# Chunked attention and a squared-ReLU FFN on one core: the opening's copies, loads and products, the mixes and bursts, and the last block's pieces are placed anew

## The chip, the cores and the metric

The kernel runs on one core of one Trainium2 chip. The time is that of one execution of the program on the device, in microseconds (us); the median of several executions is compared. In the rows PE is the matrix engine (PEld its weight loads), DVE the vector engine, ACT the scalar engine, POOL the GpSimd engine, and SP a sequencer that only issues transfers. ACT and POOL issue transfers too.

## The reference

```
q_c, k_c, v_c = (x.reshape(B, H, nc, 64, D) for x in (q, k, v))   # B, H, S, D = 8, 8, 576, 64
scores = np.matmul(q_c, k_c.transpose(0, 1, 2, 4, 3)) / np.sqrt(D)
attn = np.exp(scores - scores.max(-1, keepdims=True))
attn = attn / (attn.sum(-1, keepdims=True) + 1e-9)
x = np.matmul(attn, v_c)  ->  (4608 tokens, 512)
h = x @ w_in                                                       # 512 -> 2048
g = np.where(h >= 1, h, np.where(h <= -1, 0, (h + 1) ** 2 / 4))
out = g @ w_out                                                    # 2048 -> 512
```

Inputs and output are float32.

## The kernel before

**Tiles.** The 4608 tokens are nine tiles `t` of 512. Attention is done for two heads (a pair `g`, four to a tile) at a time: `q` and `k` are turned so that the head dimension lies on the partitions, the scores of the pair go to PSUM, DVE and ACT make the softmax, the result is turned back, and the product with `v` gives one 128-row slice of `x`. Each operand of the FFN is split into a high part and a low part (`xh` and `xl`, `gh` and `gl`, two halves of each weight), and each product is three matrix products: high by high, high by low, low by high. A product of 512 columns is the unit of the work.

**Three stages.** The opening handles tile 0: for each of its four pairs `attn_turn` (two PE transposes of 128x512 and a copy each from PSUM to SBUF), `attn_products(scores_of)`, `attn_softmax` (maximum, difference, exponential, sum, and on POOL the multiplication by the inverse sum), `attn_turn_back`, `attn_products(values_of)` and `attn_split` (ACT writes `xh`, DVE writes `xl`). The weights arrive as 64-bit words and `prepare` turns one of them into two parts with three ACT and two DVE instructions; its first ACT instruction (`Prelu`) waits for the load. Until data is there, PE multiplies the identity by itself (`warm`). Tiles 0 to 2 (`PAIRED`) then run the FFN as it stands, 16 blocks of 12 products with `w_in` and 12 with `w_out` to a tile. Blocks are numbered over the three tiles, so that block 36 is block 4 of tile 2. Tiles 3 to 8 run two at a time with seven products in place of eight (`ffn_quad`, `ffn_mixed_out`); their mixed weights are made beforehand by `mix_weights` ("mixes": DVE sums, ACT copies and seven stores to DRAM by POOL) and streamed back by POOL.

**Bursts.** The attention of later tiles is computed in bursts of two pairs. A burst is the values of one couple of pairs and the scores of the next in one group of 64x64 products. Between two bursts lies a chain: maximum, difference, exponential, sum, multiplication, a DVE transpose into `qT_both`, an SP move of `qT_both` to `aT_both` by four transfers, and DVE transposes of the next `k` and `q`. The one that writes `qT_both` cannot start before the move has read it. `PAIRS` says behind which blocks of tiles 0 to 2 a burst stands, `SCHEDULE` behind which block a mix stands and in which scratch.

**Who orders the work.** `Plan.add` collects each piece of work with an engine, an assumed duration, the buffers that it reads and writes, and an assumed delay of a transfer. `Plan.emit` runs its own estimate of all engines and writes every engine's instructions in the order that comes out, with due times counted back from the end as the rank. On the chip each engine takes its instructions in just that order.

**The end.** The last output block is made by `ffn_mixed_out` with `ending` set. Its 512 tokens go in two pieces of 256: for each piece 24 products, then per half (`c`) a DVE addition of the sum kept in SBUF (`total_of`), a DVE transpose, and four stores, two from SP and two from ACT:

```python
LAST_BANKS = a_banks, h_banks
for e, c, k in itertools.product(range(2), range(2), range(PARTS)):
    if ending:
        last_product(LAST_BANKS[e][c], k, c, slice(e * T // 2, (e + 1) * T // 2), ...)
```

Of the kernel before, what the change touches and what calls it, by code (L numbers as in the profile page):

```python
# [19 lines left out]
class Wires:  # L20


    def __init__(self):
        self.now = 0.0
        self.queues = {"pool": deque(), "sp": deque()}
        self.asked = []
# [36 lines left out]
class Plan:  # L63
# [14 lines left out]
    def __init__(self):  # L78
        self.parts = []
        self.writer = {}  # L80
        self.readers = {}
        self.written = {}
        self.behind = 0
        self.rank = []
        self.early = {}

    def add(
        self, engine, cost, emit, reads=(), writes=(), lag=0.0, columns=0, sends=0, kb=0, run=0, after=None,
    ):
        n = len(self.parts)  # L90
        needs = {self.writer[k] for k in (*reads, *writes) if k in self.writer}
# [61 lines left out]
    def run(self, filler, live):  # L153
# [33 lines left out]
        done = {None}  # L187

# [8 lines left out]
        while left or sending:  # L197
# [44 lines left out]
            n = heapq.heappop(now[e])[1]  # L242
            left -= 1
# [5 lines left out]
            times[n], self.took[n] = start, end - start  # L249
            if e == "sp":  # L250
# [5 lines left out]
            for m in range(sends):  # L256
                wires.begin(start + cost * (m + 1) / sends, "pool" if e == "pool" else "sp", n, *wire)
# [4 lines left out]
def kernel(  # L262
# [35 lines left out]
    EARLY = 2  # L298
# [12 lines left out]
        (15, EARLIER), (15, EARLIER), (15, EARLIER), (17, EARLIER), (19, OWN), (22, EARLIER), (23, RING5), (25, RING5), (28, OWN), (33, OWN), (36, LATER), (39, LATER), (41, OWN), (41, RING5), (45, RING5), (46, OWN),  # L311
# [101 lines left out]

    def load_weight(w, j):
        def emit():
            words[w, j] = dst = place("words", w, j, [P, 2 * T], U32)
            if w == "wi":
                nc.sync.dma_start(
# [5 lines left out]
            else:  # L424
                nc.sync.dma_start(out=dst, in_=w_out[j * P:(j + 1) * P, :])

        plan.add("sp", 0.57, emit, (), (f"{w}{j}_0", f"{w}{j}_1"), lag=2.5,
# [3 lines left out]
    def prepare(w, j):  # L431
# [23 lines left out]
        plan.add("dve", 0.6, join, both, (ykey,))  # L455
# [20 lines left out]
        plan.add("dve", 0.6, low, (ykey, both[0]), (both[1],))  # L476
# [50 lines left out]
    def load_heads(t, g, which="qkv"):  # L527
        for n, src, bufs in (("q", q, q_bufs), ("k", k, k_bufs), ("v", v, v_bufs)):
# [5 lines left out]
            if BATCH[t] is None:  # L534
                parts *= 2

            issuer, queue = ("act", nc.scalar) if (n, t) == ("k", 0) and g < 2 else ("sp", nc.sync)
            plan.add(
                issuer, (0.67 if t < 2 else 0.55) * parts,
# [10 lines left out]

    def attn_turn(t, g):
        for n, (name, bufs, src_bufs, dst_bufs) in enumerate(
# [6 lines left out]
            turned[n] = plan.add(  # L559
                "act", 0.48, lambda ps=ps, dst=dst: nc.scalar.copy(out=dst, in_=ps), (pkey,), (dkey,)  # L560
            )
# [85 lines left out]
    def attn_softmax(t, g):  # L647
# [26 lines left out]
        plan.add("pool", 1.05, lambda: nc.gpsimd.tensor_tensor(  # L674
# [838 lines left out]
```

## Time and profile before

| | before |
|---|---|
| median of 3 runs (lowest, highest) | 793.46 us (792.54, 793.69) |
| the profiled execution | 793.6 us |
| its span from first to last instruction | 791.8 us |
| PE busy in the span | 782.8 us (99%) |
| DVE, ACT, POOL busy | 659.9, 523.4, 178.4 us |
| granted clock of PE over the span | 0.999 of full speed |

The time holds 1.8 us beside the span. PE is busy almost throughout, but in the first 25 us much of that is `warm`, and a busy PE may also be waiting inside an instruction; so the distance between the starts of products says more than the busy time.

### The profile page before, as it was taken

To read this page: it belongs to the slowest core of one execution; us is meant where nothing else is said; L and a number is where in the kernel's file an instruction comes from. 1 tells how busy PE (TensorE), PEld (TensorE's weight loads), DVE (VectorE), ACT (ScalarE), POOL (GpSimd) and SP (SyncE) were. 2 spreads that over 40 slices of the span, in tenths; PEclk is the share of its full clock that TensorE was granted. 3 is DMA by queue.
4 is the path that set the end of the run, shared out by engine and by line. 5 is a ranking of instruction groups with operands and counts; after the bars stand their busy time and mean duration, and the time that the engine had idled before them with its cause. 6 is when DMAs were issued, how large, how long until landed. Compare 5 with 4: busy or idle time off the path is not lost.

```text
span 791.8 us, 15101 instructions
## 1 busy us (share of the span) xinstructions
PE 782.8 (99%) x5626; PEld 646.2 (82%) x5626; DVE 659.9 (83%) x1013; ACT 523.4 (66%) x903; POOL 178.4 (23%) x294
## 2 busy tenths in 40 slices
PE   9999999999999999999999999999999999999997
PEld 8788888878878888887887888888888888888886
DVE  4889998898679889998769999887699976755796
ACT  5998975444445456886579667865797658657851
POOL 1000005743234433222111112121112111211211
PEclk9999999999999999999999999999999999999999
DMA  9896869858799867898899879989766896666664
GB/s 207 221 359 152 252 136 289 290 174 234 190 277 278 219 170 232 246 299 229 225 243 240 225 210 271 273 226 241 204 198 185 220 260 207 191 192 191 183 207 106
DMA packets 254664, 177.16 MB, mean 224 GB/s; under 512 B 211968, under 2 KB 220160, under 8 KB 254592
## 3 DMA queue, kind: packets, MB, share of 16 engines
q0 software_dynamic: 33344, 117.98, 47.4%
q1 hardware_dynamic: 216992, 57.18, 32.0%
q10 hardware_dynamic: 4256, 1.05, 0.7%
q8 instruction: 44, 0.72, 0.4%
q14 instruction: 28, 0.23, 0.1%
HBM read 133.17 MB, written 38.80 MB: 217 GB/s over the span
## 4 chain that ended last, share of the span: by engine, by line
PE 83%; DVE 7%; ACT 4%; DMA 3%; SPq 1%; issue 1%; ACTq 0%; DVEq 0%
PE ps_o L1060 39%; PE ps_o L823 14%; PE ps_h L788 14%; PE ps_h L1060 12%; PE ps_a L579 2%; DMA aT_both<-qT_both 2%; PE ps_h L600 1%; DVE big_wo L1111 1%; DMA k_sb_both<-in_k_dram 1%; ACT big_wo L1110 1%; ACT big_wo L1107 1%; DMA words_wi<-in_moe_w_in_dram 1%; SPq L490 1%; SPq L722 0%; PE ps_o L600 0%
## 5 line engine op out<-in xcount | busy, mean ns | idle before, releaser
L968 POOL DMA_DIRECT2D big_wi<-mixed x144 | 76.8, 534 | 325.7 <-PE ps_o L1060 178.2
L788 PE MATMUL ps_h<-xh,parts_wi 128*128 128x512 f32 x376 | 123.9, 392 | 0.1
L823 PE MATMUL ps_o<-parts_wo,gh 128*128 128x512 f32 x384 | 119.5, 392 | 0.0
L1060 PE MATMUL ps_o<-big_wo,big_wi 128*128 128x512 f32 x396 | 95.6, 389 | 0.0
L1060 PE MATMUL ps_o<-gh,big_wi 128*128 128x512 f32 x264 | 88.6, 391 | 0.4 <-ACT big_wo L1075 0.3
L1060 PEld LDWEIGHTS ps_o<-big_wo,big_wi 128*128 128x128 f32 x396 | 74.3, 188 | 15.5
L788 PEld LDWEIGHTS ps_h<-xh,parts_wi 128*128 128x128 f32 x376 | 70.6, 188 | 16.5 <-DVE r L799 1.2
L823 PEld LDWEIGHTS ps_o<-parts_wo,gh 128*128 128x128 f32 x384 | 71.4, 188 | 15.3 <-issue 0.3
L1060 PE MATMUL ps_h<-big_wi,big_wi 128*128 128x512 f32 x312 | 75.9, 390 | 0.0
L823 PE MATMUL ps_o<-parts_wo,gl 128*128 128x512 f32 x192 | 74.8, 390 | 0.0
L788 PE MATMUL ps_h<-xl,parts_wi 128*128 128x512 f32 x188 | 73.3, 390 | 0.1
L1060 PE MATMUL ps_o<-big_wi,big_wi 128*128 128x512 f32 x282 | 70.8, 391 | 0.7 <-ACT tmp L1075 0.4
L1060 PEld LDWEIGHTS ps_h<-big_wi,big_wi 128*128 128x128 f32 x312 | 58.4, 188 | 12.2
L1167 ACT CAST big_wo<-big_wo 128x512 fp32r<-128x512 f32 x76 | 47.2, 622 | 31.6 <-PE ps_o L1060 19.9
L1060 PEld LDWEIGHTS ps_o<-big_wi,big_wi 128*128 128x128 f32 x282 | 52.6, 188 | 12.8 <-ACT tmp L1075 1.3
L1167 ACT CAST gh<-big_wo 128x512 fp32r<-128x512 f32 x76 | 47.2, 621 | 23.2 <-PE ps_o L1060 18.2
L1168 DVE TENSOR_TENSOR big_wo<-big_wo,big_wo 128x512 fp32r<-128x512 f32 x76 | 51.6, 684 | 11.6 <-ACT big_wo L1167 11.6
L1110 ACT ACTIVATE big_wo<-big_wo 128x512 f32<-128x512 f32 x96 | 59.8, 632 | 1.9
L1060 PEld LDWEIGHTS ps_o<-gh,big_wi 128*128 128x128 f32 x264 | 49.5, 188 | 12.0 <-ACT big_xl L753 0.8
L1168 DVE TENSOR_TENSOR gl<-big_wo,gh 128x512 fp32r<-128x512 f32 x76 | 51.6, 683 | 8.6 <-ACT gh L1167 8.5
L795 ACT ACTIVATE r<-ps_h 128x512 f32<-128x512 f32 x47 | 28.1, 597 | 36.4 <-PE ps_h L788 36.2
L1060 PE MATMUL ps_o<-gl,big_wi 128*128 128x512 f32 x132 | 51.4, 390 | 0.0
(269 smaller groups left out, 1648.9 us busy)
## 6 DMA issues: line engine op xcount, KB each, us to landing
big_wi<-mixed POOLq DMA_DIRECT2D x144, 512.0 KB, 4.7
big_wo<-mixed POOLq DMA_DIRECT2D x24, 512.0 KB, 4.3
words_wi<-in_moe_w_in_dram SPq DMA_DIRECT2D x16, 512.0 KB, 7.0
words_wo<-in_moe_w_out_dram SPq DMA_DIRECT2D x16, 512.0 KB, 8.8
v_sb<-in_v_dram SPq DMA_DIRECT2D x60, 128.0 KB, 4.0
q_sb_both<-in_q_dram SPq DMA_DIRECT2D x112, 64.0 KB, 3.9
k_sb_both<-in_k_dram SPq DMA_DIRECT2D x112, 64.0 KB, 3.1
mixed<-parts_wi POOLq DMA_DIRECT2D x24, 256.0 KB, 4.2
```

The lines of the kernel that those rows point to most:

```text
L490: queue.dma_start(out=dst[j * C:(j + 1) * C], in_=heads_rows(src, t, 2 * g + j).rearrange("c p d -> p c d"),)
L579: nc.tensor.matmul(out=scores[i * C:(i + 1) * C, half, n * C:(n + 1) * C], lhsT=qT[rows, at], rhs=kT[rows, at], start=True, stop=True,)
L600: nc.tensor.matmul(out=values[half][h * C:(h + 1) * C, n * C:(n + 1) * C], lhsT=v_sb[rows, of:of + C], rhs=rhs, start=True, stop=True,)
L788: nc.tensor.matmul(out=ps, lhsT=weight["wi", j][:, half, kc * P:(kc + 1) * P], rhs=x(), start=(kc == 0 and i == 0), stop=(kc == KC - 1 and ...
L795: plan.add("act", 0.48, lambda: nc.scalar.activation(out=r, in_=ps, func=AF.Relu, bias=0.5, scale=0.5), (pkey,), (rkey,))
L823: nc.tensor.matmul(out=acc, lhsT=x[:, cols], rhs=weight["wo", j][:, half, :], start=(j == 0 and i == 0), stop=(j == NF - 1 and i == 2),)
L968: nc.gpsimd.dma_start(out=place_of(tag).bitcast(F32), in_=mixed[n][:, rows, :])
L1060: nc.tensor.matmul(out=bank, lhsT=parts[part], rhs=rhs, start=fresh and begin and k == 0, stop=end and k == 2, skip_group_check=not fresh,)
L1107: plan.add("act", 0.5, lambda: nc.scalar.activation(out=r(), in_=h(), func=AF.Relu, bias=0.5, scale=0.5), (hkey,), (rkey,))
L1110: plan.add("act", 0.52, lambda: nc.scalar.square(out=r(), in_=r()), (), (rkey,))
L1167: plan.add("act", 0.52, lambda: nc.scalar.copy(out=h(), in_=x()), (key,), (hkey,))
L1168: plan.add("dve", 0.6, lambda: nc.vector.tensor_tensor(out=l(), in0=x(), in1=h().bitcast(F32), op=ALU.subtract), (key, hkey), (lkey,))
```

## The change

It changes tables and rules in six places, with no change in what is computed.

1. The copies of turned `q` of pairs 0 and 2 move from ACT to DVE (`TURNED_BY`). ACT's transfer queue loads `k` of pair 0 and `q` of pair 1 in place of `k` of both.
2. The first four FFN blocks are planned product by product, each with the operands that it reads (`APART`), not as groups of three.
3. First loads, later loads and loads of `q` and `k` of tile 1 are listed in another order.
4. `SCHEDULE`, `PAIRS`, `QUAD_BURSTS` and the order of the `w_out` mixes have other entries.
5. The planner keeps DVE instructions of `prepare` that read two SBUF operands away from POOL's arithmetic (`two_in_sbuf`).
6. The last block goes in three pieces of 256, 128 and 128 tokens. Each PSUM bank is first filled by ACT with the kept sum (`seeded`), the products add to it, and DVE transposes straight out of PSUM.

```diff
-    EARLY = 2
+    EARLY, APART = 2, 4
+    LOADED_BY = {('k', 0): 'act', ('q', 1): 'act'}
+    TURNED_BY, BACK_BY, NORM_BY = "daaadaaa", "aaaa", "pppp"
...
     SCHEDULE = (
-        (15, EARLIER), (15, EARLIER), (15, EARLIER), (17, EARLIER), (19, OWN), (22, EARLIER), (23, RING5), (25, RING5), (28, OWN), (33, OWN), (36, LATER), (39, LATER), (41, OWN), (41, RING5), (45, RING5), (46, OWN),
+        (15, EARLIER), (16, EARLIER), (19, RING5), (19, OWN), (21, EARLIER), (21, EARLIER), (21, EARLIER), (24, OWN), (24, RING5), (33, RING5), (33, OWN), (36, RING5), (41, LATER), (43, OWN), (45, RING5), (47, OWN),
     )
...
+    def copied(by, to, bank):
+        (key, dst), (pkey, ps) = to, bank
+        if by == "d":
+            return plan.add("dve", 0.6, lambda: nc.vector.tensor_copy(out=dst, in_=ps), (pkey,), (key,))
+        return plan.add("act", 0.48, lambda: nc.scalar.copy(out=dst, in_=ps), (pkey,), (key,))
...
+            if n < APART:
+                for i, reads in enumerate(((wkeys[0], hkey), (wkeys[0], lkey), (wkeys[1], hkey))):
+                    plan.add("pe", 0.227, lambda i=i, products=products: products((i,)), reads, (pkey,), columns=T)
+                continue
...
-    LAST_BANKS = a_banks, h_banks
-    LAST_SUMS = [whole(x) for x in (e_bufs[0], tmp_bufs[2])]
+    LAST_BANKS = o_banks[2:], h_banks, o_banks[:2]
+    LAST_AT = 0, 256, 384, 512
...
+            for e in range(len(LAST_BANKS) if ending else 0):
+                at = slice(LAST_AT[e], LAST_AT[e + 1])
+                for c in range(2):
+                    key, x = chunks_of(D_TAG)[c]
+                    seeded(
+                        (LAST_BANKS[e][c][0], last_tokens(e, c)),
+                        (key, lambda x=x, at=at: x()[:, at.start // Q:at.stop // Q]),
+                    )
+                for c, k in itertools.product(range(2), range(PARTS)):
+                    last_product(LAST_BANKS[e][c], k, c, at, *parts_of[k], ["late_products"])
...
-    PAIRS = {0: (6, 10, 15), 1: (7, 11), 2: (0, 4, 9, 15)}
+    PAIRS = {0: (5, 10, 15), 1: (6, 12), 2: (1, 4, 11, 15)}
```

**PE's order in the opening, in words.** There are 36 `warm` products where there were 41. Ahead of the values of pair 3, the last in tile 0, stand 14 FFN products of 512 columns where there were 12.

**ACT, late in the opening.** Seven rows in which the opening's third and fourth pair meet the weights, first of before and then of the change. `words_wi` are loads of `w_in` (the 1st to 4th have the numbers 175, 225, 259 and 296 before, 172, 207, 255 and 298 now), and the copy into `first_wi_99` is that of the attention weights of pair 2 the first time, of pair 3 the last time.

```order
L467 CAST parts_wi_382<-tmp_both 128x512
L442 ACTIVATE tmp_both<-words_wi_259 128x512
L737 CAST xh_0_0_405<-ps_a 128x2x4x64
L445 ACTIVATE words_wi_259<-words_wi_259 128x512
L442 ACTIVATE tmp_88<-words_wi_296 128x512
L684 COPY first_wi_99<-ps_o_92 128x512
L467 CAST parts_wi_432<-tmp_both 128x512
```

```order
L490 CAST parts_wi_395<-tmp_both 128x512
L465 ACTIVATE tmp_both<-words_wi_255 128x512
L766 CAST xh_0_0_405<-ps_a 128x2x4x64
L468 ACTIVATE words_wi_255<-words_wi_255 128x512
L579 COPY first_wi_99<-ps_o_92 128x512
L465 ACTIVATE tmp_88<-words_wi_298 128x512
L490 CAST parts_wi_431<-tmp_both 128x512
```

The copy of pair 3 has moved from behind the `Prelu` that waits for the 4th load of `w_in` to ahead of it. Earlier in the same queue the `Prelu` of the 2nd load now stands ahead of the cast of the 1st, and on SP that 2nd load has moved from behind `v` of pair 1 to ahead of it.

**SP, between two bursts of tile 2.** The rows show the loads of `v` for the burst behind block 32 (before) and 33 (now), the stores of tile 1's output and the move for the next burst, which in both stands behind block 36; `q_sb` and `k_sb` load for the burst after that.

```order
L521 DMA v_sb_70<-in_v_dram 128x4x64 x2
L521 DMA v_sb_71<-in_v_dram 128x4x64 x2
L851 DMA out_dram<-tmp_88 128x512
L851 DMA out_dram<-tmp_87 128x512
L851 DMA out_dram<-tmp_88 128x512
L851 DMA out_dram<-tmp_87 128x512
L722 DMA aT_both<-qT_both 32x512 x4
```

```order
L544 DMA v_sb_70<-in_v_dram 128x4x64 x2
L544 DMA v_sb_71<-in_v_dram 128x4x64 x2
L886 DMA out_dram<-tmp_88 128x512
L886 DMA out_dram<-tmp_87 128x512
L886 DMA out_dram<-tmp_88 128x512
L751 DMA aT_both<-qT_both 32x512 x4
L886 DMA out_dram<-tmp_87 128x512
```

One of the four stores has moved behind the move. On PE 84 products of 512 columns stand between these two bursts where there were 96. All copies that these stores wait for now stand ahead of the chain's sum on DVE and ahead of its exponential on ACT; one of them stood behind the transpose into `qT_both`. The other gap that got short has 99 products (block 43 to 47).

**PE, the last products.** The rows are the end of the second and last piece before, and the end of the second and all of the third piece now.

```order
L1060 MATMUL ps_h_94<-big_wo_3641,big_wo_3126 128x256 x3
L1060 MATMUL ps_h_94<-big_wo_3731,big_wo_3126 128x256 x3
L1060 MATMUL ps_h_94<-big_q_sb,big_wi_2502 128x256 x3
L1060 MATMUL ps_h_94<-big_k_sb,big_wi_2502 128x256 x3
```

```order
L1097 MATMUL ps_h_94<-big_q_sb,big_wi_2486 128x128 x3
L1097 MATMUL ps_h_94<-big_k_sb,big_wi_2486 128x128 x3
L1097 MATMUL ps_o_91<-big_wo_3611,big_wo_3115 128x128 x3
L1097 MATMUL ps_o_91<-big_wo_3716,big_wo_3115 128x128 x3
L1097 MATMUL ps_o_91<-big_q_sb,big_wi_2486 128x128 x3
L1097 MATMUL ps_o_91<-big_k_sb,big_wi_2486 128x128 x3
L1097 MATMUL ps_o_92<-big_wo_3611,big_wo_3115 128x128 x3
L1097 MATMUL ps_o_92<-big_wo_3716,big_wo_3115 128x128 x3
L1097 MATMUL ps_o_92<-big_q_sb,big_wi_2486 128x128 x3
L1097 MATMUL ps_o_92<-big_k_sb,big_wi_2486 128x128 x3
```

The 24 products of 256 columns of the last piece have become 48 products of 128 columns. The first piece keeps its 24 products of 256.

## Rows read from the trace of the kernel before

**Rows 1.** The page, part 1: busy us (share of span) and instructions.
```profile
PE 782.8 (99%) x5626; PEld 646.2 (82%) x5626; DVE 659.9 (83%) x1013; ACT 523.4 (66%) x903; POOL 178.4 (23%) x294
```
**Rows 2.** Windows: PE, PEld, DVE, ACT, POOL busy (x); clock, DMA share, GB/s.
```profile
0.00:20.00 20.00, 18.52 (x274) 17.32 (x274) 8.78 (x18) 10.78 (x19) 3.84 (x9) 1.00 0.97 208
20.00:40.00 20.00, 19.61 (x180) 15.48 (x179) 17.14 (x28) 18.49 (x34) 1.04 (x1) 1.00 0.87 222
80.00:100.00 20.00, 20.00 (x208) 16.57 (x207) 18.78 (x28) 19.75 (x37) 0.00 (x0) 1.00 0.88 248
```
**Rows 3.** Waits of PE: for whom, us in total, times, longest.
```profile
PE ps_h L1473 <- POOL ident masks.py:199: 1.4, 1, 1.4
PE ps_h L600 <- DVE r L799: 1.3, 2, 1.1
```
**Rows 4.** Timeline, opening, PE: start, us, instruction.
```profile
5.77 0.28 PE L1473 MATMUL ps_h<-ident 128*128 128x128 f32 x1
7.05 1.06 PE L1473 MATMUL ps_h<-ident 128*128 128x128 f32 x8
21.81 0.50 PE L788 MATMUL ps_h<-xh,parts_wi 128*128 128x512 f32 x1
27.11 0.69 PE L600 MATMUL ps_o<-first_wi,first_wo 64*64 64x64 f32 x32
27.74 0.50 PE L788 MATMUL ps_h<-xh,parts_wi 128*128 128x512 f32 x1
28.07 0.40 PE L788 MATMUL ps_h<-xl,parts_wi 128*128 128x512 f32 x1
```
**Rows 5.** Timeline, opening, ACT, POOL and SP: [idle before <- what ended it].
```profile
14.14 1.08 SPq L418 DMA_DIRECT2D words_wi<-in_moe_w_in_dram  x1
17.79 0.62 ACT L467 CAST parts_wi<-tmp 128x512 fp32r<-128x512 f32 x1 [0.24 <-DVE tmp L450]
19.80 0.69 ACT L442 ACTIVATE tmp_both<-words_wi 128x512 f32<-128x512 f32 x1 [0.42 <-DMA words_wi<-in_moe_w_in_dram]
21.16 0.63 ACT L664 ACTIVATE first_wo<-first_wo 128x512 f32<-128x512 f32 x1
23.51 1.04 POOL L674 TENSOR_TENSOR first_wo<-first_wo,sm_both 128x512 f32<-128x512 f32 x1 [3.53 <-DVE sm_both L671]
25.49 0.70 ACT L442 ACTIVATE tmp<-words_wi 128x512 f32<-128x512 f32 x1 [0.43 <-DMA words_wi<-in_moe_w_in_dram]
26.07 0.59 ACT L684 COPY first_wi<-ps_o 128x512 f32<-128x512 f32 x1
```
**Rows 6.** Timeline around the burst behind block 36: DVE, SP and PE.
```profile
213.63 1.22 DVE L697 TENSOR_REDUCE mx_both<-ps_a 128x16 f32<-128x1024 f32 x1 [0.48 <-PE ps_a L579]
216.79 8.29 SPq L851 DMA_DIRECT2D out_dram<-tmp  x3
222.11 1.23 DVE L724 STREAM_TRANSPOSE qT_both<-kT_both 128x1024 f32<-128x1024 f32 x1
225.18 3.93 SPq L722 DMA_DIRECT2D aT_both<-qT_both  x4
234.44 1.25 DVE L565 STREAM_TRANSPOSE qT_both<-q_sb_both 128x1024 f32<-128x1024 f32 x1 [2.79 <-DMA k_sb_both<-in_k_dram]
236.91 0.27 PE L600 MATMUL ps_h<-aT_both,v_sb 64*64 64x64 f32 x1 [1.10 <-DVE r L799]
```
**Rows 7.** Timeline of an earlier chain without a wait: DVE and SP.
```profile
184.00 1.22 DVE L697 TENSOR_REDUCE mx_both<-ps_a 128x16 f32<-128x1024 f32 x1 [0.92 <-PE ps_a L579]
195.45 2.41 SPq L722 DMA_DIRECT2D aT_both<-qT_both  x4
200.93 1.23 DVE L565 STREAM_TRANSPOSE qT_both<-q_sb_both 128x1024 f32<-128x1024 f32 x1
```
**Rows 8.** The chain that ended last, in order of time: start, us, what.
```profile
102.60 2.72 PE ps_o L823 x12
...
123.98 3.03 PE ps_h L788 x12
...
162.95 5.75 PE ps_h L788 x24
...
170.74 3.02 PE ps_h L788 x12
...
227.97 6.35 DMA aT_both<-qT_both
```
**Rows 9.** Timeline, PE: twelve full products in the FFN, and the last two pieces.
```profile
769.11 2.88 PE L1060 MATMUL ps_o<-big_wo,big_wi 128*128 128x512 f32 x12
781.56 0.88 PE L1060 MATMUL ps_a<-big_wo,big_wo 128*128 128x256 f32 x6
784.40 0.88 PE L1060 MATMUL ps_h<-big_wo,big_wo 128*128 128x256 f32 x6
```
**Rows 10.** Lines by form, weight loads: warm-up at 6.9 to 8.1 us, last pieces.
```profile
L1473 PEld LDWEIGHTS ps_h<-ident 128*128 128x128 f32 x8 | 1.0, 192 | 0.0
L1060 PEld LDWEIGHTS ps_h<-big_wo,big_wo 128*128 128x128 f32 x12 | 1.6, 189 | 0.0
```
**Rows 11.** Timeline, DVE, the last piece, and one wider transpose.
```profile
785.39 0.71 DVE L1242 STREAM_TRANSPOSE tmp<-e 128x512 f32<-128x512 f32 x1
787.44 0.42 DVE L1069 TENSOR_TENSOR tmp_both<-ps_h,big_wo 128x256 f32<-128x256 f32 x1 [0.51 <-PE ps_h L1060]
787.90 0.45 DVE L1239 STREAM_TRANSPOSE tmp<-tmp_both 128x256 f32<-128x256 f32 x1
```
**Rows 12.** DMA issues, 784 to 792 us: KB each, median us to landing.
```profile
out_dram<-tmp ACTq DMA_DIRECT2D x4, 64.0 KB, 2.1
```

More of the change, by code (lines that the diff above doesn't have):

```diff
@@ L187, in run @@
         done = {None}
+        port_free = 0.0
         def fill():
@@ L242, in run @@
             n = heapq.heappop(now[e])[1]
+            if e == "dve" and n in self.two_in_sbuf and start < port_free:
+                late = [n]
+                while now[e] and late[-1] in self.two_in_sbuf:
+                    late.append(heapq.heappop(now[e])[1])
+                n = late.pop() if late[-1] not in self.two_in_sbuf else late.pop(0)
+                for m in late:
+                    heapq.heappush(now[e], self.rank[m])
+                if n in self.two_in_sbuf:
+                    start = port_free
             left -= 1
@@ L249, in run @@
             times[n], self.took[n] = start, end - start
+            if e == "pool" and not sends:
+                port_free = end
             if e == "sp":
@@ L256, in run @@
             for m in range(sends):
-                wires.begin(start + cost * (m + 1) / sends, "pool" if e == "pool" else "sp", n, *wire)
+                wires.begin(start + cost * (m + 1) / sends, e, n, *wire)
         return times
@@ L784, in ffn_in, with products @@
             lkey, xl = x_part("xl", t, kc)
-            def products(kc=kc, xh=xh, xl=xl):
-                for i, (half, x) in enumerate(((0, xh), (0, xl), (1, xh))):
+            def products(some, kc=kc, xh=xh, xl=xl):
+                for i in some:
+                    half, x = ((0, xh), (0, xl), (1, xh))[i]
                     nc.tensor.matmul(
@@ L1154, in emit @@
             parts = [w()[:, at_ * HALF + c * P:at_ * HALF + (c + 1) * P] for at_ in range(2)]
-            product(bank[:, :T // 2], parts, (h()[:, at], l()[:, at]), True, k == 0, k == PARTS - 1)
-        plan.add("pe", 0.345, emit, (skey, hkey, lkey, *before), (key, "last_products"), columns=3 * T // 2)
+            product(bank[:, :at.stop - at.start], parts, (h()[:, at], l()[:, at]), False, k == 0, k == PARTS - 1)
+        size = at.stop - at.start
+        plan.add("pe", 0.03 + 0.63 * size / T, emit, (skey, hkey, lkey, *before), (key, "last_products"), columns=3 * size)
     def ffn_mixed_out(t, half, at):
@@ L1209, in ffn_mixed_out @@
             if ending:
-                for e in range(2):
-                    store_last(t + last[2], last[1], e, chunks_of(last[0]))
+                for e in range(len(LAST_BANKS)):
+                    store_last(t + last[2], last[1], e)
             if half == 1 and last and not ending:
```

103 lines of the change are left out of this document (49 added, 54 removed).

## The prediction

> **What bounds the kernel now.** I read the page's busy times first. PE is busy 782.8 of 791.8 us [rows 1], at full clock in the stages that I read [rows 2], so the steady part can give nothing but its few holes. The FFN products follow each other every 0.226 us: twelve of them take 2.88 us from first start to last end, (2.88 - 0.39) / 11, where 0.39 us is what a lone one shows [rows 4, 9]. The change neither adds nor drops a product of 512 columns. So the time can move in three places only: the opening, where PE has too little to do and fills up with warm-ups; waits of PE in the middle; and the end behind the last full product. The list of PE's waits is short. Beside the start (1.4 us on the identity) the only entry over half a microsecond is 1.3 us, two times on DVE [rows 3]. The timeline of the opening and that of the end give the rest.
>
> The sum is made against the profiled execution, 793.6 us (span 791.8 us and 1.8 us around it). That is 0.1 us over the median of the runs, 793.46 us, less than the sum can resolve, so I don't correct for it. A measurement of this kernel tells about 0.2%, 1.6 us, from no change.
>
> **The opening: 0.85 us less.** ACT is what the opening goes through: from 20 to 40 us it is busy 18.49 of 20 us, while in the first 20 it is busy 10.78 [rows 2]. The two copies that move to DVE are done before 12 us, where both engines have room (DVE 8.78 of 20), so I cost that edit at nothing; without that room a copy would cost up to the 0.59 us of such an ACT copy [rows 5]. The same holds for the rule on POOL and two SBUF operands: it matters beside four POOL multiplications only, and DVE's idle time covers it.
>
> What counts is where ACT waits for loads. Before, the `Prelu` of the second load starts at 19.80 as that load lands, and the one of the fourth at 25.49 in the same way [rows 5]. The second load is now issued ahead of 256 KB of `v`; at 208 GB/s in that stretch [rows 2] it lands 1.2 us sooner, at about 18.6. The price: in ACT's order this `Prelu` now stands ahead of the cast of the first load, which ran at 17.79 and now runs at 19.2. I walk on with the distances that the rows show. Behind the `Prelu` come the cast, a copy and the second word step, three steps of some 0.6 us, and then the exponential of pair 3 at 21.0 instead of 21.16. The POOL multiplication of that pair stood at 23.51 because two DVE steps of 0.6 us, which wait for the casts and for the weights, ran between the exponential and its sum; one of them is ahead now, so 22.95. Before, the copy of its attention weights could have followed at about 25.45 (the multiplication's 1.04 us, four PE transposes and gaps), and it was held up by the `Prelu` at 25.49 until 26.07 [rows 5]. Now it stands ahead of that one and starts at about 25.1. The values of pair 3 started on PE at 27.11 [rows 4]. Now eight FFN products stand between the turn of pair 3 and its values, so they start not at 25.9 but at about 26.7: 0.4 us earlier, with two more products behind PE, 0.45 us. Together 0.85 us, and from there PE had no hole to speak of and has none now.
>
> Bounds: nothing at all if the second load lands no sooner than 19.80, for then casts, exponential and all behind them move back by 1.2 us and eat the gain. At most 1.6 us, if all of the five warm-up calls fewer (two PE instructions each, ten at 0.111 us; the spacing is below) and a further 0.5 us of PE's waiting there turn into work.
>
> **The middle: 1.3 us less.** The long wait, 1.10 us at 236.91 [rows 6], has a story in its rows. SP stood in three stores of output from 216.79 to 225.08. The move of `qT_both`, ready at 223.34 (222.11 + 1.23), stood behind them until 225.18 and then took 3.93 us to issue. DVE, in order, sat 2.79 us in front of the transpose that overwrites `qT_both` until 234.44, and what PE needed was behind it. That row names a load of `k`, but the chain of waits has the last transfer of the move, 227.97 + 6.35 = 234.32 [rows 8]. In an earlier chain the maximum starts at 184.00 and the last transpose ends at 202.16, 18.2 us; in the long one it took from 213.63 to 235.69, 22.1 us [rows 6, 7]. In the new order the last store stands behind the move and the copies for the others come early in the chain, so SP should be free when `qT_both` is ready. The price is a shorter cover: 84 products in place of 96 stand between the bursts, 84 x 0.226 = 19.0 us in place of 21.7. A chain of 18.2 us fits with under 1 us to spare. I take that case, and so the whole entry of 1.3 us as gone. Bounds: at most 2.2 us less, if three small holes go too: on the chain of waits groups of 12 and 24 products take 3.03, 5.75 and 3.02 us where twelve without a hole take 2.72, 0.3 us too long each [rows 8]; if the chain takes 22.1 us again, PE waits 3.1 us in its place, so 1.8 us more than before. Two mixes now stand behind block 33, in the same gap; their stores share the wires with the move, which is what speaks for that case. The other tables move work that lies beside PE's products; the rows show engines with room (POOL 178.4 us, ACT 523.4 us of the span [rows 1]), and I cost it at nothing. Only in the first 100 us is there little of it (ACT 19.75 and DVE 18.78 of 20 us between 80 and 100 [rows 2]), and if a weight came late there PE would wait; that is in the range.
>
> **The end: 1.6 us more.** Before, the two pieces start at 781.56 and 784.40 [rows 9]: 24 products of 256 columns in 2.84 us, 0.118 us each, a little over half of 0.226. Now 24 of them are followed by 48 of 128 columns. No row shows this product at 128 columns. If the spacing went on halving it would be 0.059 us and 48 would take 2.83 us, as the 24 did. If each product must wait for the load of its own weights, 128 columns cost what 256 do. Three things speak for the second. After a pause the second product starts 0.33 us behind the first (27.74, 28.07) and the first takes 0.50 us instead of 0.39, as if the load, otherwise hidden behind the product ahead, took 0.10 to 0.11 us [rows 4]. The record of a load is 189 ns whatever the product's width [rows 10]. And the nearest row at 128 columns, the warm-up's plain float32 products, has eight in 1.06 us, (1.06 - 0.28) / 7 = 0.111 us apart, where 0.28 is a lone one, with loads of 192 ns [rows 4, 10]. I take 0.111: 48 x 0.111 = 5.33 us in place of 2.84, 2.5 us more.
>
> Against it stand two savings. The addition of the last half goes, 0.46 us from its start at 787.44 to that of the transpose at 787.90, and the transpose shrinks from 256 to 128 columns: 0.71 us at 512 and 0.45 at 256 make 0.31 at 128, 0.14 less [rows 11]. Together 0.60 us. The last stores carry half the bytes; at 2.1 us to landing for 64 KB [rows 12] I take 0.3 us off, between nothing and half a microsecond. The ACT seeds cost nothing: they are ready once the sum is, ahead of the first piece, and ACT had nothing to do there; only those of the third piece wait for the transposes of the block ahead, and PE reaches it more than 5 us later. Were that cover gone, one seed of some 0.4 us would be seen. So 2.5 - 0.60 - 0.30 = 1.6 us more. Bounds: 0.9 us less (0.059 each), 2.2 us more (0.118 each, no saving at the stores).
>
> The Trainium skill (TensorE: Matmul & The Clock Gate, LDWEIGHTS (loading the stationary operand)) gives a load's time as its columns divided by 1.2, in ns: 107 ns for 128 columns, so 48 would take 5.1 us, and the end would be 1.4 us longer (estimate). It speaks against this change, and the pause of 0.10 to 0.11 us in the rows agrees with it.
>
> **Sum.** 793.6 - 0.85 - 1.3 + 1.6 = 793.05, or 793.1 us.
>
> **Rivals.**
> - *The weight loads don't bind at 128 columns.* Then the end gains 0.9 us: 793.6 - 0.85 - 1.3 - 0.9 = 790.55 us, faster. For it: 256 columns cost nearly half of 512, with no floor seen yet; against it: the pause and the warm-up row. The Trainium skill (the same page, Back-to-back issue gap) has a sustained 81 ns at 128 columns; then 48 would take 3.9 us, the end 0.2 us more, and the total would be 791.6 us (estimate). No run here shows it yet.
> - *The shorter gap between the bursts behind blocks 33 and 36 comes up short.* If DVE again waits in front of the overwriting transpose and the chain takes 22.1 us, 793.1 + 3.1 = 796.2 us, slower. It decides from a chain of 19.0 us on; at 20.6 us the sum passes the measurable bound. For it: two mixes in the gap, 18.2 us in the good chain; against it: the store behind the move.
> - *The opening doesn't gain,* since ACT's queue waits for the second load as long as before: 793.95 us, no change. For it: the cast of the first load is now behind that wait.
> - *All small holes of tiles 1 and 2 go too:* 792.2 us, no change by the bound.
>
> **How the numbers follow.** The forecast has 0.40, the loads that don't bind 0.16, the short gap 0.22, the opening without gain 0.12, the holes 0.10. Faster by over 0.2%: the first rival and a part of the last with a better opening, 0.21. Slower: the short gap and some of the forecast's own spread, where a weight comes late in the first 100 us, 0.28. Within: 0.51. The forecast alone spans 791.9 to 794.6 us. The range reaches to the first two rivals, since both signs count: 790.4 to 796.2 us.
>
> **What would show it.** Opening: the last values of tile 0 on PE start before 27 us, with the copy ahead of them no longer behind the `Prelu`. Middle: no wait on DVE's r over 0.5 us, and the maximum to the last transpose in under 19 us behind block 33. End: the products of 128 columns 0.11 us apart, the first piece's start to the last product's about 8.2 us (5.7 before), then a transpose of 0.31 us. The forecast is wrong if the last pieces run at 0.06 to 0.08 us, or if PE shows a new wait at a burst.

## The result, and the profile after

The changed kernel takes 798.35 us in the median of 6 runs (796.81 to 801.22), the kernel before 793.0 beside it: ratio 1.0069, interval 1.0053 to 1.0085. It is slower by 5.4 us and lies above the forecast's range. The profiled execution took 798.6 us, span 796.8.

Part 1 of the page after, where TensorE has 3 us more to do than in [rows 1] and 5 us more span; the windows that answer to [rows 2], and four around 220 us:

```profile
PE 785.8 (99%) x5640; PEld 649.9 (82%) x5640; DVE 659.8 (83%) x1014; ACT 525.6 (66%) x907; POOL 178.7 (22%) x294
```
```profile
0.00:20.00 20.00, 18.00 (x268) 16.76 (x268) 10.64 (x21) 9.47 (x16) 4.12 (x9) 1.00 0.94 199
20.00:40.00 20.00, 19.54 (x176) 15.46 (x176) 15.48 (x26) 19.50 (x38) 1.05 (x1) 1.00 0.89 264
...
215.00:221.00 6.00, 2.49 (x129) 2.23 (x128) 1.30 (x3) 2.19 (x4) 2.58 (x4) 0.93 1.01 351
221.00:227.00 6.00, 6.00 (x15) 4.71 (x15) 2.45 (x2) 1.06 (x1) 0.00 (x0) 0.50 0.72 220
227.00:240.00 13.00, 13.00 (x58) 10.76 (x58) 10.86 (x17) 6.22 (x10) 1.66 (x3) 1.00 0.45 127
```

From 215 to 221 us TensorE is busy 2.49 of 6 us. From 221 to 227 it is always busy, yet starts 15 products where 13 us later have 58: the granted clock is 0.50, the lower level of 1.2 GHz. The waits of TensorE, where [rows 3] had 1.3 us on DVE's r, and its timeline there:

```profile
PE ps_a L607 <- issue: 3.5, 1, 3.5
PE ps_h L1504 <- POOL ident masks.py:199: 1.4, 1, 1.4
PE ps_h L818 <- ACT parts_wi L490: 0.6, 1, 0.6
```
```profile
216.13 0.99 PE L607 MATMUL ps_a<-kT_both,qT_both 64*64 64x64 f32 x54
220.63 0.47 PE L607 MATMUL ps_a<-kT_both,qT_both 64*64 64x64 f32 x2 [3.51 <-issue]
221.04 1.22 PE L858 MATMUL ps_o<-parts_wo,gh 128*128 128x512 f32 x2
222.06 0.63 PE L858 MATMUL ps_o<-parts_wo,gl 128*128 128x512 f32 x1
```

In the burst behind block 33, TensorE stops with its last scores to do and stands for 3.51 us. "Issue" says that it waited for nothing that the profile shows. Then two FFN products take 1.02 us from start to start (221.04, 222.06), 0.51 each, and later 0.43, in place of 0.226. Counted to 226.8 us, some 14 products lose 0.2 us each, 2.8 us. With the stop that is 6.3 us, more than the whole loss. Nothing like it is in [rows 3]; but one row of the same kind stood in the trace before, in another burst, and I had not read it:

```profile
498.62 0.79 PE L579 MATMUL ps_a<-kT_both,qT_both 64*64 64x64 f32 x35 [0.31 <-issue]
```

The queues of the page have a line that fits: q8, "instruction", 45 packets, 0.74 MB. TensorE began 11,280 weight loads and products, about 250 for each packet; from 600 to 790 us, 7 packets and 1,715 such instructions, 245. So I read q8 as what brings TensorE its instructions. The queues in two stretches of the changed kernel (packets, MB, share), 189.9 to 217.1 us, and 217.1 to 220.6:

```profile
q0 software_dynamic: 780, 2.68, 30.7%
q1 hardware_dynamic: 8845, 1.38, 29.5%
```
```profile
q0 software_dynamic: 263, 0.87, 62.2%
q1 hardware_dynamic: 402, 0.51, 39.8%
q8 instruction: 1, 0.02, 1.9%
```

No packet starts for 27 us, and one while TensorE stands. A burst is 256 instructions in 1.9 us; as many take 29 us among FFN products (128 x 0.226). A packet that comes late is felt in a burst or soon behind one. The trace shows 3,488 weight loads and products ahead of this burst, 1,744 of each. The expectations below have 3,584, since they count four instructions for a transposing product where the trace shows two; the distances between places, on which the experiments rest, are the same by either count.

Where TensorE stands settles the reading of q8. Counted in the trace with its semaphore instructions (11,477 in all, 255 for each of the 45 packets), TensorE had begun 3,777 instructions at this stop, 13 x 256 + 449, after 13 packets. The twenty traces of this document have 19 stops of 0.2 us or more that end by "issue" behind the first 10 us. At each of them the count is exactly 256 for each packet that has come, plus 449, and TensorE goes on 1.2 to 1.7 us behind the end of the next packet. In no trace does it get further without that packet. So these are stops for want of instructions. The runs below were planned without this count; they test the reading from other sides and ask what makes the packet late.

### The profile page after: what moved, and what is told of

It reads as the page before. It is cut to its first block, busy times and chain, and to the rows that moved or that the text cites. A ratio compares the mean times of both kernels' runs of the same rounds, so it can differ in the third digit from the quotient of the medians.

```text
span 796.8 us, 15154 instructions
## 1 busy us (share of the span) xinstructions
PE 785.8 (99%) x5640; PEld 649.9 (82%) x5640; DVE 659.8 (83%) x1014; ACT 525.6 (66%) x907; POOL 178.7 (22%) x294
## 4 chain that ended last, share of the span: by engine, by line
PE 83%; DVE 5%; ACT 4%; issue 3%; DMA 3%; POOL 1%; SPq 1%; DVEq 0%; POOLq 0%; ACTq 0%
PE ps_o L1097 39%; PE ps_o L858 15%; PE ps_h L818 14%; PE ps_h L1097 13%; PE ps_a L607 1%; PE ps_h L628 1%; POOL mixed L914 1%; DMA mixed<-tmp_both 1%; ACT big_wo L1144 1%; DMA words_wi<-in_moe_w_in_dram 1%; ACT big_wo L1147 1%; DMA q_sb_both<-in_q_dram 1%; DVE big_wo L1106 1%; SPq L513 1%; DVE big_wo L1148 1%
```

## Experiments

Times are medians beside runs of the kernel before, ratios with their intervals. **Theory:** the packet came late ("fetch"). Rivals are a wait for data that the profile doesn't name, the transfers around 213 us, and the opening or the end as the true cost.

**The place in the stream.** This product, 16 times ahead of the first warm-up:

```diff
+            nc.tensor.matmul(out=bank[:C, :C], lhsT=ident[:C, :C], rhs=ident[:C, :C], start=True, stop=True)
```

> The changed kernel with 16 more warm-up products of 64 columns at the very start of TensorE's program, and nothing else; they write a bank that the warm-up products overwrite. They move everything behind them by the same number of instructions in TensorE's instruction stream (64 by the trace's count: each of these f32 products shows as two weight loads and two products). Theory 'fetch': the stop of 3.5 us at 217.1 us, whose end the profile puts down to nothing it shows, is TensorE without instructions, because a packet of its instruction queue came late; it hangs on where in the stream the burst begins. Then the stop is gone or under 1 us, the clock stays at its upper level there, and the time falls by 3.5 + 2.8 us to 792.1 (791 to 794; no change to the kernel before). Rival 'data': the scores waited for a tile, a bank or a transfer that the profile does not name. Then nothing that it waits for is moved, the stop stays where it is, and the time stays 798.4 (ratio 1.007).

795.55 us, 1.0052 (1.0034 to 1.0070). The stop in the burst is gone, though no data moved: "data" falls. But the time is 3.5 us over what I expected. The warm-ups cost 2.1 us in the opening. The profiled execution took 798.63 us and another 799.3, the other four 795.1 to 795.8; in the profile a next wait came forward, with the clock at 0.55 from 227 to 230 us. ACT's copy into `tmp` waited for a store that SP had issued at 218.04, and TensorE for the copy (ACT's row, then TensorE's):

```profile
226.16 0.59 ACT L880 COPY tmp<-ps_o 128x512 f32<-128x512 f32 x1 [6.25 <-DMA out_dram<-tmp]
```
```profile
226.79 1.22 PE L858 MATMUL ps_o<-parts_wo,gh 128*128 128x512 f32 x2 [2.86 <-ACT tmp L880]
```

**Transfers taken away.** Only the entries of `SCHEDULE` that differ are shown, here and in the run behind it:

```diff
-(33, RING5), (33, OWN), (36, RING5)
+(33, RING5), (34, OWN), (36, RING5)
```

> The changed kernel with the second of the two mixes behind block 33 made behind block 34. It takes transfers out of the stretch of 213 to 218 us (in the changed kernel's trace POOL issues six moves of 256 KB there, SP two stores and two loads) and puts one pair of FFN-out products ahead of the burst. Theory 'crowd': the packet of instructions stood behind these transfers; with fewer of them the stop is gone and the time is 792 to 794. Rival 'edge': what decides is the burst's place in TensorE's instruction stream alone, whatever the transfers do; the burst moves by some ten instructions, the stop stays between 2 and 3.7 us, and the time stays 796 to 798.4. Rival 'data' (a wait for something the profile does not name, tied to the mix): gone as by 'crowd', but then the run with 16 more warm-ups keeps it.

799.8 us, 1.0096 (1.0080 to 1.0112); a stop of 4.0 us. Three moves fewer change nothing.

```diff
+(35, RING5), (35, OWN), (36, RING5)
```

> The changed kernel with both mixes behind block 33 made behind block 35: the six moves of 256 KB that POOL issues at 213 to 217 us in the changed kernel, just ahead of the burst behind block 33 and into it, come some 6 us later; loads, stores and the place of the burst in TensorE's program stay. The shifted run showed the packet of instructions going out at 205.4 us, when the DMA engines were 0.35 busy, and no stop; in the changed kernel and in the run with one mix moved it went out only at 218, a microsecond after TensorE had stopped. Theory 'crowd' (the packet stands behind the transfers of 206 to 217 us): it goes out earlier than 215 us, the stop is under 1 us, the clock stays at its upper level, and the time is 792 (791 to 794.5). Rival 'edge' (the burst's place in the instruction stream alone decides, whatever the transfers): the stop is 3 us or more and the time 796 to 799. Rival 'loads': the q and k loads of 202 to 213 us make the backlog by themselves; then the stop stays as by 'edge', and the packet goes out at 217 to 218.

796.42 us, 1.0045 (1.0029 to 1.0060); a stop of 2.7 us, the packet still gone out only behind its start (217.5 us, the stop from 216.8), and one of 0.95 us in a later burst. The clock stayed at 1.00 this time. The six moves are not what holds it up.

**The parts of the change.** In turn: the tables back as before (the diff of `SCHEDULE`, `PAIRS`, `QUAD_BURSTS` and the order of `wo` reversed), two pieces in place of three (below), the tables alone in the kernel before, the end alone there, that end in two pieces, and the changed kernel with the diff of the end reversed.

```diff
+    LAST_BANKS = o_banks[2:], h_banks
+    LAST_AT = 0, 256, 512
```

> The changed kernel with the four tables of the middle as before (places of the mixes, places of the pairs' bursts, order of the wo blocks, places of the later bursts): what is left of the change is the new opening and the new end. By the prediction's terms: 793.0 - 0.85 (opening) + 1.6 (end) = 793.75, with the wait of 1.3 us behind block 36 back in the trace and no stop at 217 (ratio 1.001). Rival 'opening or end': one of these cost the 5.4 us; then the time is 796.5 or more and the stretch from 100 to 600 us is as long as before.

796.31 us, 1.0049 (1.0034 to 1.0063), a miss by 2.6 us. No stop in the burst, but 1.8 us of waiting for DVE's r at 95.8 us, which neither kernel has: the new opening and the old tables don't fit together. So a part's worth can't be read off by taking it alone.

> The changed kernel with the seeded last block in two pieces of 256 columns in place of three. 48 products of 128 columns, 0.111 us apart in the changed kernel's trace (5.33 us), become 24 of 256 columns, 0.118 apart (2.83 us): 2.5 us less; behind the last product the transpose is of 256 columns (0.45 for 0.31 us) and the stores are of 64 KB (2.1 for 1.8 us to landing), 0.45 us more. Sum: 798.4 - 2.05 = 796.3 (ratio 1.0043), the stop at 217 us as in the changed kernel. Rival 'columns': the third piece costs nothing, because columns alone bind; then 798.4 + 0.45 = 798.8.

796.49 us, 1.0050 (1.0035 to 1.0066). As expected it is better than the changed kernel, by about 1.5 us (2.05 expected), with a stop of 4.0 us.

> The kernel before with the four tables of the middle as changed, old opening and old end. Theory: the tables alone bring the crowd and the stop. The waits behind blocks 21 and 36 go (-1.3 us), the stop and the low clock behind block 33 come (3.5 + 2.8 us, or the same loss one step later as in the shifted run, 3.0 us and the clock): 793 - 1.3 + 5 = 796.7 (ratio 1.005, 1.003 to 1.007). Rival 'interplay': the stop needs the new opening's count of instructions or its transfers; then only the gain is left, 791.7 (ratio 0.998).

796.26 us, 1.0042 (1.0027 to 1.0056): the time as expected, the cause not. Its burst starts 20 instructions past the place and has no stop; it waits 1.6 us for DVE's r, in two waits, and 1.3 us by "issue" at another place, among FFN products, after 17 x 256 + 449 instructions:

```profile
281.75 0.73 PE L823 MATMUL ps_o<-parts_wo,gh 128*128 128x512 f32 x2 [1.29 <-issue]
```

> The kernel before with the new end alone (three seeded pieces), every instruction up to the last tile as before. By the changed kernel's trace, from its last product of 512 columns to the end 12.13 us against 10.47 before: +1.67, so 793 + 1.67 = 794.7 (ratio 1.0021); the prediction's term was +1.6. Rival: in the changed kernel the end was long because of what stood ahead of it; alone it costs nothing (ratio 1.000).

795.1 us, 1.0031 (1.0020 to 1.0041). Alone too the end costs something near what the prediction said: 2.2 us by the medians, at its upper bound, and 1.85 us by the trace (12.09 us from the start of the first piece to the span's end, 10.24 before).

> The kernel before with the seeded end in two pieces of 256 columns. By the prediction's terms the products cost what they cost before and VectorE's two adds go (0.46 + 0.14 us): 793 - 0.6 = 792.4 (ratio 0.9992). Rival 'late stores': in the changed kernel with two pieces the time from the last product of 512 columns to the end was 11.9 us, 1.4 more than before, because the stores of the blocks before the last one came later and the last stores stood behind them; then 794.4 (ratio 1.0018).

794.52 us, 1.0019 (1.0010 to 1.0029), as the rival of the late stores has it: from the end of the last product to the span's end it is 5.9 us where it was 4.4. Which store is the cause was not tested. Seeding in itself gains nothing.

> The changed kernel with the end as before: two pieces of 256 columns, added to the totals by VectorE behind their products. If the end is a cost of its own (+1.67 us by the changed kernel's trace, +2.2 by the run with the end alone): 798.4 - 1.9 = 796.5 (ratio 1.0045), with the stop at 217 us as in the changed kernel. Rival: what is late ahead of the end hides it; then 798.4 (ratio 1.007).

795.41 us, 1.0030 (1.0011 to 1.0050), and a surprise. The profiled execution took 788.1 us at a mean clock of 0.999, without any wait of TensorE but that on the identity; the other eleven took 793.1 to 798.3 at 0.994 to 0.998. All six executions of the changed kernel show 0.994 to 0.996, and those of the kernel before 0.998 to 1.0. So I took the stop for a matter of chance from one execution to the next, with bad odds; none of those eleven was profiled.

**Leaving out 16 loads of q and k ahead of the burst** (one pair of heads is computed from older rows):

```diff
-                lambda load=load, dst=dst, src=src, queue=queue: load(dst, src, t, g, queue),
+                lambda load=load, dst=dst, src=src, queue=queue, left_out=n in 'qk' and t == 4 and g < 2: (
+                    None if left_out else load(dst, src, t, g, queue)
+                ),
```

> The changed kernel without the 16 loads of q and k (64 KB each) that SP issues at 201.5 to 213 us, for the pair of heads two bursts later, which is computed from older rows instead; every other instruction of every engine stands where it stood. Theory 'loads' (the packet of instructions is due some 300 instructions ahead of running dry, at about 209 us, and stands behind the backlog that begins with these loads): it goes out before 214, the stop of TensorE in the burst is under 1 us, the clock stays at its upper level, and the time is 792 (791 to 794). Rival 'edge' (the burst's place in the stream alone decides): stop of 3 us or more, time 796.5 to 799.

796.11 us, 1.0037 (1.0016 to 1.0058). Three executions took 789.8 to 791.3 us, one of them profiled and without a stop, nine 794.6 to 799.7. So I took this kernel and the one with the old end a second time:

> A second profile of the changed kernel without the 16 loads of q and k. Its first two executions took 789.8 us at clock 1.0, a third 791.3, the other nine 794.6 to 799.7 at 0.994 to 0.999. If this profile falls on one of those nine: theory 'loads' in its strong form (these loads make the backlog) says that the loss is elsewhere than in the burst at 217 us; theory 'edge and chance' (the packet has little time there in any case, and these loads only make it late more often) says that the stop of 3 to 4 us is there again, the packet late by 7 us or more.

> A second profile of the changed kernel with the end as before. Its first profile fell on the one execution of twelve without a stop (788.1 us, clock 0.999); the other eleven took 793.1 to 798.3 us at a mean clock of 0.994 to 0.998. Theory 'fetch': in an execution of those the packet of instructions goes out 7 us or more after TensorE began the 303rd instruction ahead of running dry, TensorE stops in the burst at 217 us for 2 to 4.5 us, 'issue' by the profile, and nearly all of the 5 to 10 us between the two executions lies in that stop and in the low clock behind it. Rival 'many small': the slow executions lose it in several places of under a microsecond each.

Without the loads it now took 796.8 us and stopped, 3.5 us here and 0.9 us in a later burst. The packet started at 217.8 us; in the first profile, without a stop, it started at 211.5. TensorE's timeline, and windows ahead of the stop, whose last two numbers are the DMA engines' share and GB/s:

```profile
215.74 0.99 PE L609 MATMUL ps_a<-kT_both,qT_both 64*64 64x64 f32 x54
220.18 0.32 PE L609 MATMUL ps_a<-kT_both,qT_both 64*64 64x64 f32 x2 [3.45 <-issue]
```
```profile
203.00:206.00 3.00, 3.00 (x15) 2.49 (x14) 2.95 (x5) 1.27 (x3) 1.41 (x2) 1.00 0.21 87
206.00:209.00 3.00, 3.00 (x15) 2.49 (x14) 0.90 (x2) 1.23 (x2) 2.06 (x4) 1.00 0.82 198
209.00:212.00 3.00, 3.00 (x15) 2.49 (x14) 0.69 (x1) 0.62 (x1) 0.00 (x0) 1.00 0.66 239
```

The old end took 789.1 us and didn't stop. Its engines were busier, and the packet went out ahead of the burst's end, at 214.05 (windows, then the queues from 213 to 216.6 us, then TensorE behind the burst without a gap):

```profile
206.00:209.00 3.00, 3.00 (x15) 2.45 (x15) 1.01 (x2) 1.23 (x2) 2.17 (x4) 1.00 1.11 263
209.00:212.00 3.00, 3.00 (x15) 2.49 (x14) 0.69 (x1) 0.62 (x1) 0.00 (x0) 1.00 0.94 218
```
```profile
q8 instruction: 1, 0.02, 1.7%
```
```profile
215.85 1.00 PE L607 MATMUL ps_a<-kT_both,qT_both 64*64 64x64 f32 x56
216.78 0.73 PE L858 MATMUL ps_o<-parts_wo,gh 128*128 128x512 f32 x2
```

Busy DMA engines and no stop, calmer ones and a stop: in its strong form "loads" falls as well.

**The burst moved.** Old end, opening and tables as changed:

```diff
-    PAIRS = {0: (5, 10, 15), 1: (6, 12), 2: (1, 4, 11, 15)}
+    PAIRS = {0: (5, 10, 15), 1: (6, 12), 2: (2, 5, 11, 15)}
```

> Opening and tables as changed, end as before, but the two pairs of heads whose bursts stand behind blocks 33 and 36 are put behind blocks 34 and 37: in program order 48 more instructions of TensorE stand ahead of the first of these bursts (3,632 weight loads and products for 3,584), and the packet that it needs is due that much further ahead of it. Theory 'fetch': no stop in that burst in nearly all executions, and the times gather where the old end's one execution without a stop was: 789 (788 to 791.5), ratio 0.996, faster than the kernel before. Rival 'crowd': whatever stands in the queue of transfers behind these bursts, a store or a load, is late anyway, as in the shifted run; then 793 to 796.

790.96 us, 0.9982 (0.9971 to 0.9992), all eleven executions from 790.5 to 792.6. This version beats both kernels. TensorE begins its 3,777th instruction at 222.2 us, 216.9 in the changed kernel, so that even a packet as late as the one there (218.2 to 219.3 us) would have come in time; it came at 212.3. The longest wait of TensorE behind the start is 0.4 us:

```profile
PE ps_h L1507 <- POOL ident masks.py:199: 1.4, 1, 1.4
PE ps_h L818 <- DVE r L834: 0.8, 2, 0.4
```

> The changed kernel, its own end included, with the two bursts behind blocks 33 and 36 put behind 34 and 37. The run with these bursts and the old end took 791.0; the new end costs 1.7 to 2.2 us: 792.9 (792 to 794), ratio 1.000 (0.999 to 1.002): the whole loss of the change, but for the end, is the place of that burst. Rival: the loss stays at 795 or more.

793.31 us, 1.0011 (1.0002 to 1.0019). The whole change with this one table moved is 0.1% over the kernel before.

> The same with the two mixes behind block 33 made behind block 35, so that their six moves come behind the burst. Theory 'fetch': again no stop, 788 to 791.5. If what is left of the loss comes from the transfers around the burst, it is at least 1 us faster than the run without this; if mixes behind 35 only push work into the stretch behind it (the run with them behind 35 had new waits of 1.1, 1.0 and 1.2 us at 239, 350 and 500 us), it is 1 to 3 us slower.

794.17 us, 1.0023 (1.0013 to 1.0033): new waits of 1.0 us for a move and for DVE. The mixes belong at 33.

> Opening and tables as changed, but the two mixes behind block 33 made behind block 35, the first 16 warm-up products made as two of 64 columns each (64 more instructions ahead of everything, as in the shifted run, for at most 0.7 us), and the end as before. From the run with the mixes behind 35 (796.4): - 2.9 (its stop, gone by the shift) - 2.2 (the end, by the run with the end alone) + 0.5 (warm-ups) = 791.8, ratio 0.999; range 790.5 to 794. If the wait moves on to the next thing in the queue of transfers, as in the shifted run, 794 to 795 (ratio 1.002).

796.99 us, 1.0051 (1.0036 to 1.0065): a miss. The finer warm-ups put off the first FFN product to 24.6 us (20.36 in the changed kernel), "issue" had 1.7 us in a later burst, after 27 x 256 + 449 instructions, and two waits on DVE had 1.6 and 1.5 us:

```profile
436.60 0.46 PE L607 MATMUL ps_a<-kT_both,qT_both 64*64 64x64 f32 x16 [1.66 <-issue]
```

**The place alone**, in the kernel before: the line of the first experiment, 7 and 14 times.

> The kernel before with 7 more warm-up products of 64 columns at the very start (28 instructions of TensorE), and nothing else. They put the burst behind block 32 where the changed kernel's burst behind block 33 stands: 3,584 weight loads and products ahead of it in program order, 3,556 without them. Theory 'edge': TensorE stops in that burst, at about 214 us, for 2 to 4.5 us by 'issue', its clock falls behind it in the executions in which the stop is long, and the time is 792.6 + 0.9 (the products, by the shifted run's 2.1 us for 16) + 3 to 6 = 796.5 to 799.5. Rival 'tables': it takes the transfers of the new tables; no stop, 793.5 (ratio 1.001).

793.73 us, 1.0014 (1.0003 to 1.0025). No stop in that burst (first two rows); in the profiled execution, the slowest of its eleven, one of 1.6 us in another (last row) and one of 0.7 us in the opening:

```profile
215.59 1.00 PE L579 MATMUL ps_a<-kT_both,qT_both 64*64 64x64 f32 x56
216.52 0.73 PE L823 MATMUL ps_o<-parts_wo,gh 128*128 128x512 f32 x2
```
```profile
PE ps_a L579 <- issue: 1.6, 1, 1.6
```

> The kernel before with 14 such products: the burst behind block 32 stands at 3,612, the one behind block 5 at 1,538 (two past the sixth multiple of 256, where the burst of the changed kernel stood on the fourteenth). Theory 'edge': no stop behind block 32; 792.6 + 1.8 = 794.4 (ratio 1.002), or up to 4 us more if the burst behind block 5 now stops for the same reason. Rival 'more is worse' (the products themselves cost the time, not the place): twice what the run with 7 loses, 798 or more, without a stop anywhere.

796.14 us, 1.0040 (1.0028 to 1.0052): no stop over 0.8 us; 2.6 us of warm-ups and waits of 1.3 and 0.9 us for DVE's r. "Edge" in its strong form falls: the place does not make the stop by itself.

## Why the prediction was wrong

**The middle, the step that failed.** "The other tables move work that lies beside PE's products [...] and I cost it at nothing" was wrong. A row of `PAIRS` puts a burst to a place in TensorE's own program where a late packet of instructions stops it, 3.5 us, and the clock behind it 2.8 us. I named "a new wait at a burst" as what would make me wrong, but gave it no price, for I looked for it among tiles and engines alone.

Shown: TensorE stands where its instructions run out, 449 behind the last multiple of 256, and goes on when the next packet has come. The stop goes away with 64 instructions more ahead of the burst. With the burst alone 48 instructions on, neither profile has a stop and all 23 executions have clocks of 0.998 to 1.0 (with the mixes moved as well, no stop in the profile and 0.996 to 1.0 in eleven). Of the kernel without the 16 loads, one profile has the packet at 211.5 us and no stop, the other has it at 217.8 and stops of 4.4 us, and 7 us lie between them (789.8, 796.8). That executions without a profile lose their time in this stop is inferred from times and clocks. Not settled is why the packet is late so often in the changed kernel at this place and not in the kernel before at the same place: neither the moves, nor the loads, nor the busy share of the DMA engines, nor the place alone decides it.

What I did price came out. The wait of 1.3 us is gone. In the run with the old end and no stop, the chain behind block 33 takes 18.1 us, from 217.02 to 235.12, under the 19 us that I named, and the shorter gap is enough: that rival falls. In the changed kernel itself the chain takes 20.9 us (221.14 to 242.05), part of it at the low clock. Its size was too small, though. The last block starts at 776.08 us in that run and 781.56 before [rows 9], 5.5 us earlier, of which the opening has 0.7 (and the profile before, 793.6 us, is 1 us over the median of the later runs): the small holes went too, as the rival of the holes has it, and more than its 2.2 us. With the burst behind 34 the last block starts at 778.50, 3.1 us earlier.

**The opening: right, the size within its bounds.** Predicted 0.85. The 61st product of 512 columns, counted in the timeline, starts at 38.41 us where it was 38.96: 0.55 less, between 0.3 and 1.4 in other profiles with this opening. The values of pair 3 start at 26.81 (27.11 in [rows 4]; 26.7 predicted), and the copy ahead of them, at 25.52, no longer stands behind the `Prelu` at 26.00 [rows 5]. One term was mis-sized: the `Prelu` of the second load came 0.7 us sooner, at 19.12, and not 1.2, and the exponential of pair 3 not at all sooner (21.26, before 21.16; 21.0 predicted). The multiplication on POOL still came 0.23 us sooner (23.28), and the copy, in its new place, 0.55:

```profile
26.81 0.69 PE L628 MATMUL ps_o<-first_wi,first_wo 64*64 64x64 f32 x32
```
```profile
19.12 0.67 ACT L465 ACTIVATE tmp_both<-words_wi 128x512 f32<-128x512 f32 x1 [0.72 <-DMA words_wi<-in_moe_w_in_dram]
...
25.52 0.59 ACT L579 COPY first_wi<-ps_o 128x512 f32<-128x512 f32 x1 [0.50 <-PE ps_o L571]
26.00 0.66 ACT L465 ACTIVATE tmp<-words_wi 128x512 f32<-128x512 f32 x1
```

**The end: right.** Predicted 1.6 us. From the start of the first piece to the span's end it was 10.24 us (781.56 to 791.8), now 11.88 (784.92 to 796.8): 1.64 more. TensorE, then DVE:

```profile
784.92 0.88 PE L1097 MATMUL ps_o<-big_wo,big_wo 128*128 128x256 f32 x6
...
788.38 0.50 PE L1097 MATMUL ps_h<-big_q_sb,big_wi 128*128 128x128 f32 x3
788.71 0.50 PE L1097 MATMUL ps_h<-big_k_sb,big_wi 128*128 128x128 f32 x3
789.05 0.83 PE L1097 MATMUL ps_h<-big_wo,big_wo 128*128 128x128 f32 x6
...
792.73 0.50 PE L1097 MATMUL ps_o<-big_k_sb,big_wi 128*128 128x128 f32 x3
```
```profile
793.34 0.32 DVE L1273 STREAM_TRANSPOSE e<-ps_o 128x128 f32<-128x128 f32 x1 [1.04 <-PE ps_o L1097]
```

Groups of three start 0.33 and 0.34 us apart, 0.112 a product (0.111 predicted); first start to last end is 8.3 us (784.92 to 793.23, "about 8.2" to the last product); the transpose takes 0.32 us (0.31). Of the Trainium skill (TensorE: Matmul & The Clock Gate), the 107 ns that LDWEIGHTS (loading the stationary operand) gives for 128 columns agree with these rows within 5 ns; the sustained 81 ns under Back-to-back issue gap are not reached here. The rival whose loads don't bind falls.

Without the stop the change comes near the sum and doesn't meet it. With its bursts moved it takes 793.31 us, where 793.05 was worked out, but that the two are close is luck: the kernel before took 792.46 beside it, so it is 0.8 us slower, and the sum had 0.55 us faster.

## What to carry to other kernels

A short row that ends by "issue" in a burst of small products is a warning: there TensorE uses up its instructions some fifteen times as fast as among long ones, and a late packet of them stands in the open. A table that moves such a burst moves it in the instruction stream too, so try it one block further before believing or dropping the change. And look at several executions with their clocks: the first profile of the version with the old end, at 788.1 us, is 7 us under its median.

## What the runs showed of the hardware

- The instructions of TensorE come by a queue of the same DMA engines as the data, one packet of 16 KB for 256. In 19 stops of 0.2 to 4.0 us TensorE had begun exactly 256 for each packet that had come, plus 449, and went on 1.2 to 1.7 us behind the end of the next one.
- One program stops in one execution and not in another (without the 16 loads: 796.8 and 789.8 us).
- Behind the stop of 3.5 us the granted clock was 0.50 for 6 us of full work; behind that of 2.7 us it stayed at 1.00.
- Warm-up products of 64 columns at the start of the program put the 61st product of 512 columns off by 2.1 us for 16 in the changed kernel, and by 2.6 us for 14 in the kernel before. In the profile with 7 it is 2.5 us, with a stop of 0.7 in it, so the cost doesn't go by their number; why not was not tested.
